# Gated linear attention and a gMLP block on one core: another start of batch 0, one decay exponential and one mask operation per chunk, a new order table

## The chip, the cores and the metric

One core of a Trainium2 chip runs the whole program. It has a matrix engine (TensorE, PE in the profile), three engines for elementwise work (VectorE or DVE, ScalarE or ACT, GpSimd or POOL), and queues for transfers (issued here by SyncE, SP). The metric is the device time of one execution in microseconds. Three runs of the kernel before took 138.06, 138.46 and 139.54 us, so the median is 138.46 us.

## The reference

There are 4 batches, 8 heads, 768 tokens and a head size of 48. An attention with a decaying state comes first, then a gated block with a product along the tokens:

```python
for t in range(S):
    state = alpha[:, :, t, :, None] * state + einsum('bhd,bhe->bhde', k[:, :, t], v[:, :, t])
    y[:, :, t] = einsum('bhd,bhde->bhe', q[:, :, t], state)
x = y.transpose(0, 2, 1, 3).reshape(B, S, H * D)          # [4, 768, 384]
h = maximum(x @ w_in, 0)                                  # [4, 768, 1024]
u, v = h[..., :512], h[..., 512:]
v_n = (v - mean(v)) / sqrt(var(v) + 1e-6)
v_s = einsum('ts,bsd->btd', w_spatial, v_n) + b_spatial[None, :, None]
out = (u * v_s) @ w_out                                   # [4, 768, 384]
```

## The kernel before

The tokens of each batch are cut into 6 chunks of 128, which gives 24 chunks numbered 0 to 23. For one chunk the kernel takes the logarithm of alpha (ACT), sums it along the tokens with triangular matrices of ones (PE), takes exponentials of the sums (ACT), scales k and q with them (POOL and DVE), turns both with PE and copies them out of PSUM (the tile `kqT`), forms the scores of the chunk (PE), multiplies them by the causal mask (DVE, into `ptm`), and forms y from the masked scores, v and the old state (PE). A state update (PE, then DVE and POOL) leads to the next chunk. The decay of a whole chunk is one number per head and feature. PE sums it beside the other sums, and ACT takes its exponential (`ebc`, into `bc` or `bcq`).

Chunks come in three forms. A single chunk has one token in each partition. A pair (`pair`) loads two chunks at once, with two tokens in each partition; a group of four (`four_chunks`) loads four tokens a partition, which makes longer pieces for the transfers. Two tuples say where the forms stand: `PAIRS` and `QUADS` hold numbers of chunk pairs (number j is chunks 2j and 2j+1). Here batch 0 is a group of four followed by a pair, batch 1 a group of four followed by two singles, and batches 2 and 3 are singles.

Behind the attention the x of a chunk (`xT`) meets `w_in`. PE makes u and v, ACT or DVE apply the maximum, DVE takes the statistics of v, a small shift is computed, and ACT or DVE write the normalised `vn`. The spatial product takes `w_spT` and `vn`, DVE adds the bias, POOL multiplies with u, and PE multiplies by `w_out`.

No loop sets the order of this work. Each step is recorded as an operation with its engine, what it needs, and how many PSUM banks it takes. A table of words, `PLAN`, then gives the order in which all of them are issued. `P62@0:512#0` means: operation 62 on PE (D is DVE, A is ACT, G is POOL, S is SyncE), which takes bank 0, with 512 columns of a matmul on constant data issued ahead of it into bank 0 (called junk below). `replay` walks through the table. Each engine works through its own operations in this order, and waits on counters of other engines where data or banks need it. So an instruction that waits holds up everything behind it on its engine.

The eight banks of PSUM are eight tiles before, one for each bank. The lines that the change touches stand below by their numbers in the profile: L836 and L944 are the scores, L843 and L949 the masks, L586 the masks of a pair, L700, L901 and L471 the sums of the decay, L915, L725 and L504 its exponential, L1084 the shift and L1092 and L1096 the normalised v, L178 and L180 copies, L189 and L393 products on DVE or POOL, L1005 the products of the gMLP block, and L242 the junk matmuls.

Of the kernel before, what the change touches and what calls it, by code (L numbers as in the profile page):

```python
# [21 lines left out]
class Op:  # L22


    def __init__(self, key, engs, emit, deps, take, pe):
        self.key, self.engs, self.emit, self.take, self.pe = key, engs, emit, take, pe
        self.deps = [d for d in deps if d is not None]
        self.done = False


class Slot:
# [11 lines left out]
D2 D0 D4 D1 G9 G11 G5 G6 D3 S56 S57 S59 S58 A60 S12 S169 S170 A61 S275 S171 D8 P62@0:512#0:512#0:512#0 P66@1 P67 P63  # L43
P70@2 P71 P74@3 P75 A68 A64 D79 G82 P91@4,5 P52@6 A69 A72 A76 G7 A78 A92 A84 A65 G88 G87 A73 A77 D85 D90 D81 D93 D53
D83 D80 P103@6,4,5,7:512#7:424#7 P94@0,1 D86 D104 D89 D106 G13 P97@6,2:192#2 D98 A95 P100@3,0 D101 A96 P117@3,6:376#1
P115@4,1 A99 G107 G14 A15 A173 D102 D109 P128@0,2 D119 D118 P174@5 A116 A122 A176 P130@6,4 S16 D132 D131 S172 A135
P175@1 A129 P120@3 P54@2 G110 G105 P136@0,4 A121 A178 A55 G111 G108 P133@6 G181 A180 A134 G184 A179 D112 A177 D138
P123@7,3 P141@2 S20 G279 G280 G281 G17 G19 G18 D124 D125 P151@6 P187@7,4 P126@3 S23 S277 S276 D185 A152 A127 G186 G183
G113 G114 D182 P190@5,6 A189 A192 A142 P144@3 D137 P139@4 D188 D191 A140 G22 G21 D153 D143 P199@6,5 P196@2,7 P162@4
A283 A145 P290@0 A163 P154@1 P160@3 A282 A291 A155 D200 D201 D198 D197 D164 P193@4 A161 P156@7 A157 A165 D194 D146  # L50
P158@5 A159 G195 P202@1,2 P203 S26 A204 A147 D166 P293@4 P37@5,7 D38 P34@3,6 G24 S278 S387 S399 G25 S506 S29 D35
P207@1 D148 D208 D36 A39 A292 P205 P284@7 P40@3,5 A206 A285 A167 G10 D42 P210@2 D149 D150 D41 S388 S389 D168 D209 S401
S400 P287@5 P223@6 P219@3 P221@1 A211 A294 A224 A288 D212 A286 A220 A213 D298 D304 A289 A295 D214 D222 D215 A216
P225@6 P233@2 P217@3 P229@7 P237@0 A218 A28 D301 G300 G27 D307 G297 P226 D227 G303 G306 P43@3,5 D45 P230 P234 D231
D235 A296 A44 P46@4,6 P309@5,1 D311 P238 P49@7,3 D50 D51 A48 A47 A310 P312@2,6 P318@1,4 P315@5,7 P249@3 P250 A313 A319
A317 A299 A314 A302 D316 D320 D239 G236 D251 P341@4,1 P335@7,5 P245@0 P246 G305 G308 D336 D342 G232 P321@7,6,3,2 G240
G228 D343 D322 A510 G33 D337 D324 D247 P253@4 P333@7,1 P254 P241@5 P242 G323 A391 A403 A30 A340 A334 A32 G325 P392@0
D255 P348@7,6 D243 D327 D350 A393 P344@4 A394 P338@5 G31 G328 D397 D330 D349 G396 P404@3 A345 A339 A405 A406 P257@1
A395 S495 S390 A258 P260@4 P359@2 S402 G407 G248 G326 G329 S494 S560 P346@0,7 D408 P354@3,5 P410@1,6 A360 D331 A347
A353 A411 D356 D355 P362@2 G252 G398 P351@7 A352 P357@3 D412 S508 S497 S509 P421@6,1 P416@5,0 D361 S496 S507 S562 S550  # L60
S548 S611 S561 S551 S549 A358 A363 D418 D423 P511@7 P369@3 P413@0 P374@2 P380@1 D414 D417 A261 A512 P378@0 D422 A498
D364 A375 A564 P263@5 P499@6 G244 G332 G409 G256 A370 A379 A513 D371 G415 A500 A501 P419@0 P424@3 A425 G517 G505 G503
D381 D382 D516 G515 A420 P266@2 P269@4 A502 A365 A383 A270 D366 D504 P429@0 P426@1 P438@3 P440@6 D384 A368 A430 A427
P436@4 A437 A441 A385 D264 D439 P272@0 D367 D267 D428 D431 D386 P521@1 P372@4 A514 A273 P565@6 P376@2 A377 A432 A552
P442@7 A568 P529@0 D443 D522 P456@3 D433 D434 A435 A566 A567 D373 P452@7 P553@1 P518@2,5 A519 A554 A556 D520 A555 P457
D458 D530 D570 G569 G523 G557 G459 P444@4 P445 P448@5 D446 P453 D454 P468@6 P449 D558 D450 P533@7,4 P524@2,0 P572@1,3
D525 G451 G455 P472@5 P469 P460@2 P473 D526 D534 D535 G531 G447 D474 S623 A559 P575@7 D576 A573 P461 S625 S612 S563
A615 D470 D462 P616@4 P527@5 P536@1 A627 S613 A574 P579@7,3 P588@6,0 G577 A617 A528 D589 A618 A537 P628@5 A629 A571
G475 P538@2 A630 P464@1 S624 S614 S730 S718 S721 S626 S720 G620 D621 D581 D580 S733 S732 P476@6 G631 G578 P541@3
P584@7 A539 A619 A542 P465 S784 S719 A477 D632 P634@5,4 D590 A636 D466 D585 S731 A722 P591@3 S786 S772 S785 S773 S835  # L70
S774 A592 S787 S775 G622 G532 P582@1 A583 D635 D540 P637@7 P482@6 A633 A483 P723@5 G586 G471 D638 G639 A724 P645@3,4
P640@0,2 D543 G463 G587 P479@7 P604@6 P596@1 D646 D642 D641 A734 A726 D647 G729 G467 A605 A741 G727 P593@3 P600@6 A594
# [16 lines left out]

PAIRS = (2,)
QUADS = (0,3)
PLAIN = (0, 2)
IDLE = 16

SPLIT = ()
SMALL = ()


SUMS = (
# [30 lines left out]
def kernel(  # L132
# [134 lines left out]
    def op(key, engs, emit, deps=(), take=(), use=(), pe=None):  # L267
# [3 lines left out]
        for s in list(take) + list(use):  # L271
            s.users.append(o)
# [15 lines left out]
    def zeros(n):  # L288
        def emit(_):
            if n == 0:  # L290
# [5 lines left out]
                for t in bcs:  # L296
                    nc.vector.memset(t, 0.0)
# [967 lines left out]
```

## Time and profile before

| what | value |
|---|---|
| median of three runs | 138.46 us |
| profiled execution, first to last instruction (span) | 137.9 us |
| PE busy | 130.1 us (94%) |
| DVE busy | 120.2 us (87%) |
| ACT busy | 107.7 us (78%) |
| POOL busy | 86.6 us (63%) |
| moved by DMA | 28.66 MB, mean 208 GB/s |

The page gives no own time of the profiled execution beyond its span; the span is the time from its first to its last instruction. It lies 0.56 us below the median of the runs. Busy times are sums over the span, so engines overlap. A group's row holds its line, engine, operation, output and inputs with their shapes, the count, the busy time in us with the mean ns of one instruction, and the idle time of the engine ahead of it.

### The profile page before, as it was taken

What the parts mean: (1) busy time and instruction counts of PE and PEld (TensorE: products, weight loads), DVE (VectorE), ACT (ScalarE), POOL (GpSimd) and SP (SyncE); (2) the same over time, 40 slices, a digit from 0 to 9 for tenths busy, and PEclk for the clock granted to TensorE, in tenths of its full rate; (3) what the DMA queues carried; (4) which work ended last, traced back from release to release, by engine and by line L of the source; (5) the groups of instructions that cost most, each with busy time, mean ns of one, the idle gap of its engine ahead of it and who ended that gap; (6) DMA issues with size and microseconds to landing.
All of it is one profiled execution on the core that took longest, in us unless ns stands there. A gap on an engine that the chain in (4) does not pass through costs nothing.

```text
span 137.9 us, 5298 instructions
## 1 busy us (share of the span) xinstructions
PE 130.1 (94%) x2108; PEld 79.4 (58%) x2122; DVE 120.2 (87%) x300; ACT 107.7 (78%) x261; POOL 86.6 (63%) x146
## 2 busy tenths in 40 slices
PE   6999998999999999799999999999999999999990
PEld 3365555565566556466657676656576765566560
DVE  6259999989989999899899999997999999974960
ACT  3476998999999799699997989999865796953040
POOL 7355899993499799761079989520799841004550
PEclk9999999999999999999999999999999999999999
DMA  3999999499989788699999898999960597101064
GB/s 88 370 372 381 344 349 361 106 373 382 355 162 281 159 168 165 124 186 188 193 204 201 164 209 156 189 186 216 213 134 5 187 349 270 63 0 57 0 233 172
DMA packets 76521, 28.66 MB, mean 208 GB/s; under 512 B 63056, under 2 KB 74960, under 8 KB 76496
## 3 DMA queue, kind: packets, MB, share of 16 engines
q1 hardware_dynamic: 76464, 28.32, 77.8%
q8 instruction: 16, 0.26, 0.8%
q14 instruction: 9, 0.07, 0.2%
q0 software_dynamic: 32, 0.00, 0.0%
HBM read 23.60 MB, written 4.72 MB: 205 GB/s over the span
## 4 chain that ended last, share of the span: by engine, by line
PE 60%; DMA 19%; POOL 8%; issue 3%; SPq 3%; ACT 3%; DVE 0%; POOLq 0%; ACTq 0%
PE bank L1005 43%; DMA raw_w<-in_moe_w_spatial_dram 6%; DMA kc<-in_k_dram 5%; DMA raw_w<-in_moe_w_out_dram 4%; DMA ac<-in_alpha_dram 4%; PE bank L960 3%; SPq L883 3%; PE bank L944 2%; PE bank L988 2%; PE bank L416 2%; POOL w_row L180 2%; POOL kt L189 2%; PE bank L932 1%; PE bank L898 1%; POOL state L189 1%
## 5 line engine op out<-in xcount | busy, mean ns | idle before, releaser
L1005 PE MATMUL bank<-w_spT,vn 128*128 128x384 bf16 x192 | 35.6, 327 | 0.0
L189 POOL TENSOR_TENSOR gT<-vs,uT 128x384 bf16<-128x384 f32 x28 | 25.7, 933 | 14.1 <-DVE vs L1152 14.1
L189 POOL TENSOR_TENSOR kt<-kc,binv 128x384 bf16<-128x384 f32 x22 | 20.2, 928 | 22.3 <-ACT binv L908 15.2
L1005 PEld LDWEIGHTS <-vn 128*128 128x128 bf16 x192 | 17.5, 98 | 11.2 <-issue 0.3
L1005 PE MATMUL bank<-w_in,xT 128*128 128x512 bf16 x58 | 17.4, 380 | 1.6 <-ACT xT L178 0.7
L1005 PE MATMUL bank<-xT,w_in 128*128 128x384 bf16 x96 | 18.7, 326 | 0.0
L1005 PE MATMUL bank<-w_out_sb,gT 128*128 128x384 bf16 (+1 forms) x100 | 18.4, 320 | 0.0
L1152 DVE TENSOR_TENSOR vs<-bank,bsp_bc 128x384 f32<-128x384 f32 x31 | 16.3, 549 | 2.4 <-PE bank L1005 2.3
L949 DVE TENSOR_TENSOR ptm<-bank,mask 128x512 bf16<-128x512 f32 x28 | 17.9, 682 | 0.5 <-PE bank L944 0.3
L178 ACT COPY kqT<-bank 128x512 bf16<-128x512 bf16 (+1 forms) x20 | 15.0, 793 | 3.1 <-PE bank L988 1.9
L1067 DVE BATCH_NORM_STATS2 stats<-v_sb 128x6 f32<-128x512 bf16 x24 | 16.4, 683 | 0.6 <-ACT v_sb L184 0.5
L184 ACT ACTIVATE v_sb<-bank 128x512 bf16<-128x512 f32 x20 | 11.7, 597 | 2.0 <-PE bank L1005 1.7
L184 ACT ACTIVATE uT<-bank 128x384 bf16<-128x384 f32 x27 | 12.4, 494 | 0.7 <-PE bank L1005 0.6
L1005 PEld LDWEIGHTS <-w_in 128*128 128x128 bf16 x96 | 9.0, 97 | 6.7 <-DVE ptm L949 0.3
L189 DVE TENSOR_TENSOR qt<-qc,bank 128x384 bf16<-128x384 f32 x24 | 12.6, 545 | 0.2 <-DMA qc<-in_q_dram 0.2
L1005 PEld LDWEIGHTS <-gT 128*128 128x128 bf16 x100 | 9.2, 98 | 5.8
L178 ACT CAST xT<-bank 128x384 bf16<-128x384 f32 x23 | 10.4, 482 | 1.1 <-PE bank L416 0.8
L843 DVE TENSOR_TENSOR ptm<-bank,mask 128x512 bf16<-128x512 f32 x16 | 10.3, 683 | 0.2 <-PE bank L836 0.2
L242 PE MATMUL bank<-junk 128*128 128x512 f32 (+3 forms) x14 | 8.8, 763 | 1.0 <-DVE junk L1231 1.0
L1005 PEld LDWEIGHTS <-xT 128*128 128x128 bf16 x72 | 6.2, 97 | 6.2 <-ACT xT L178 1.2
L178 ACT COPY raw_w<-bank 128x384 f32<-128x384 f32 x8 | 3.8, 479 | 7.3 <-PE bank L1005 7.2
L393 DVE TENSOR_TENSOR zs<-bank,state 128x384 f32<-128x384 f32 x16 | 8.8, 548 | 0.5 <-PE bank L932 0.4
(162 smaller groups left out, 264.3 us busy)
## 6 DMA issues: line engine op xcount, KB each, us to landing
ac<-in_alpha_dram SPq DMA_DIRECT2D x14, 192.0 KB, 4.4
kc<-in_k_dram SPq DMA_DIRECT2D x14, 192.0 KB, 4.4
qc<-in_q_dram SPq DMA_DIRECT2D x14, 192.0 KB, 4.4
vc<-in_v_dram SPq DMA_DIRECT2D x14, 192.0 KB, 4.2
raw_w<-in_moe_w_spatial_dram SPq DMA_DIRECT2D x3, 768.0 KB, 7.8
out_dram<-raw_w SPq DMA_DIRECT2D x11, 192.0 KB, 2.1
out_dram<-o_sb SPq DMA_DIRECT2D x9, 192.0 KB, 2.0
ac<-in_alpha_dram SPq DMA_DIRECT2D x2, 768.0 KB, 6.7
```

The lines of the kernel that those rows point to most:

```text
L178: nc.scalar.copy(out=out, in_=in_)
L184: nc.scalar.activation(out=out, in_=in_, func=AF.Relu)
L189: ENG[eng].tensor_tensor(out=out, in0=in0, in1=in1, op=ALU.mult)
L242: nc.tensor.matmul(out=banks[n][:, 0:cols].rearrange("p (a b) -> p a b", a=4), lhsT=junk, rhs=junk[:, None, 0:cols // 4].to_broadcast([128 ...
L393: lambda _: nc.vector.tensor_tensor(out=zs[i % 3], in0=tp(), in1=state[(i - 1) % 3], op=ALU.add),
L843: nc.vector.tensor_tensor(out=ptm[n2][:, ci, s], in0=banks[sl.bank].rearrange("p (hp t) -> p hp t", hp=HP), in1=mask[:, 3][:, None, :].to_ ...
L883: nc.sync.dma_start(out=t[x].rearrange("p hp s d -> p (hp s) d"), in_=src[b, :, c * C:c * C + C, :].rearrange("h s d -> s h d"))
L949: nc.vector.tensor_tensor(out=ptm[n2][:, ci, s], in0=banks[sl_p[s].bank].rearrange("p (hp t) -> p hp t", hp=HP), in1=mask[:, 2][:, None, : ...
L960: nc.tensor.matmul(out=place(to, 3 * hp + (0, 1, 1, 2)[x]), lhsT=heads(vb, hp, x), rhs=ptm[n2][:, ci, x // 2, hp, :], start=(turn == 0), s ...
L1005: nc.tensor.matmul(out=ps, lhsT=lhsT, rhs=rhs, start=first and n == 0, stop=last and n == len(pairs) - 1)
L1067: nc.vector.bn_stats(out=stats[tt % 2], in_=v_sb[n2][:, tt, :])
L1152: nc.vector.tensor_tensor(out=vs[d], in0=banks[sl.bank][:, 0:TH], in1=bsp_bc[:, th, :], op=ALU.add)
```

## The change

Eight things change together.

- Batch 0 begins with a pair (chunks 0 and 1), and its other four chunks are one group of four with four tokens a partition: `PAIRS` goes from (2,) to (0,), `QUADS` from (0,3) to (1,3), `PLAIN`, which says how the sums are formed, from (0, 2) to (0, 1). The loads follow this split. Batches 1 to 3 keep their forms.
- The decay of a chunk is laid out on all 128 partitions. A matmul of `own_half` and `off_half` puts -1024 where the entries of the other head belong, so that one exponential gives a zero there; before, two exponentials of 64 partitions wrote the two halves of a tile that held zeros.
- One DVE instruction masks a chunk's scores in both of their banks, with 1024 elements a partition; before, two did 512 each.
- PSUM is one tile of 8 banks, and a bank is a view into it. The mask's operand is the view from the lower bank of the two to the higher, with a step.
- The shift of the layernorm is computed only for slices whose `vn` is written by ACT. That is 2 of 24 by the new table; before ACT wrote 6, and the shift was computed for all 24.
- Memsets of `bc` and `bcq` go, and those of `own_half` and `off_half` come.
- The broadcast of the spatial bias is recorded as needing the sums of chunk pair 0 where it needed those of pair 1.
- The order table is new throughout, with other banks; junk columns go from 3040 to 3600.

```diff
+D47 D48 D50 P227 D228 P302@3,0 P308@2,5 P305@7,4 A303 S271 G229 D306 D307 P242@1 P243 D244 G221 S29 A309 P328@2,4 D329
+P333@7,3 D334 A380 A304 A310 A392 P238@6 P234@0 G292 G298 P235 D236 A295 G301 P314@2,4,5,1 D315 G33 D317 A485 A31 A32
...
-PAIRS = (2,)
-QUADS = (0,3)
-PLAIN = (0, 2)
+PAIRS = (0,)
+QUADS = (1, 3)
+PLAIN = (0, 1)
+FAR = -1024.0
...
-    banks = [pp.tile([128, 512], FP32, name=f"bank{n}") for n in range(8)]
+    psum = pp.tile([128, 8, 512], FP32, name="bank")
+    banks = [psum[:, n, :] for n in range(8)]
...
+    def both_banks(slots):
+
+        lo, hi = (sl.bank for sl in ranked(slots))
+        return psum[:, lo:hi + 1:hi - lo, :]
...
+                nc.vector.memset(own_half.bitcast(FP32), 0.0)
+                nc.vector.memset(off_half, 0.0)
+                for s in range(2):
+                    nc.vector.memset(own_half[32 * s:32 * s + 1, 64 * s:64 * s + 64], 1.0)
+                    nc.vector.memset(off_half[32 * s:32 * s + 1, :, 1 - s:2 - s], FAR)
...
+    def decays(cm, n, parts):
+
+        width = 2 * n * HP
+        nc.tensor.matmul(
+            out=cm[:, DM:DM + width], lhsT=own_half, rhs=off_half[:, 0:n * HP, :].rearrange("p a s -> p (a s)"),
+            start=True, stop=False)
+        of = ones_col if n == 1 else (halves_of if n == 2 else quarters_of).rearrange("p c s -> p (c s)")
+        for hp in range(HP):
+            for x, la in enumerate(parts):
+                nc.tensor.matmul(
+                    out=cm[:, DM + 2 * n * hp:DM + 2 * n * hp + 2 * n], lhsT=la[:, hp].rearrange("p s d -> p (s d)"),
+                    rhs=of, start=False, stop=(hp == HP - 1 and x == len(parts) - 1))
...
             def ebc(_):
-                for s in range(2):
-                    nc.scalar.activation(out=bc[half(s), :, s], in_=banks[sl_c.bank][half(s), DM:DM + HP], func=AF.Exp)
+                nc.scalar.activation(
+                    out=bc, in_=banks[sl_c.bank][:, DM:DM + 2 * HP].rearrange("p (hp s) -> p hp s", s=2), func=AF.Exp)
...
-            for s in range(2):
-                def mk(_, s=s):
-                    nc.vector.tensor_tensor(
-                        out=ptm[n2][:, ci, s], in0=banks[sl_p[s].bank].rearrange("p (hp t) -> p hp t", hp=HP),
-                        in1=mask[:, 2][:, None, :].to_broadcast([128, HP, 128]), op=ALU.mult)
-
-                op(("ms", i, s), "DVE", mk, [("sc", i), ("y", 2 * j - 4), ("y", 2 * j - 3), ("one",)], use=[sl_p[s]])
+
+            def mk(_):
+                nc.vector.tensor_tensor(
+                    out=ptm[n2][:, ci], in0=both_banks(sl_p).rearrange("p s (hp t) -> p s hp t", hp=HP),
+                    in1=mask[:, 2][:, None, None, :].to_broadcast([128, 2, HP, 128]), op=ALU.mult)
+
+            op(("ms", i), "DVE", mk, [("sc", i), ("y", 2 * j - 4), ("y", 2 * j - 3), ("one",)], use=sl_p)
...
             for x in (tt - 1, tt):
+                if engine_of[made[("vn", b, x)].n] != "ACT":
+                    continue
                 nc.vector.tensor_scalar(
...
-        made[("bb", th)].deps.append(made[("cum", 1, 1)])
+        made[("bb", th)].deps.append(made[("cum", 0, 1)])
```

Of the table the diff shows the two new lines with chunks 6 and 7 of batch 1: operation 328 is the scores of chunk 6 in banks 2 and 4 and 329 their mask, 333 and 334 are those of chunk 7 in banks 7 and 3, and 238 is a spatial product into bank 6.

How the instructions stand is shown at three places. In these rows a name ends with the buffer's number in the program; `bank4_68` is bank 4 before, and `bank_64` is the one PSUM tile after. A wait on a counter of another engine stands in brackets.

The first place is the scores of chunks 6 and 7 (`kqT` times `kqT`) on PE and the spatial product (`w_spT` and `vn`) behind them. The kernel before, from the last spatial product ahead of the scores:

```order
L1005 MATMUL bank3_67<-w_spT_90,vn0_140 128x384
L836 LDWEIGHTS kqT1_111 [waits DVE_49]
L836 MATMUL bank4_68<-kqT1_111 128x128 [waits Activation_49]
L836 LDWEIGHTS kqT1_111
L836 MATMUL bank1_65<-kqT1_111 128x128
...
L836 MATMUL bank7_71<-kqT1_111 128x128 [waits Activation_49]
L836 LDWEIGHTS kqT1_111
L836 MATMUL bank5_69<-kqT1_111 128x128
...
L1005 LDWEIGHTS vn0_140
L1005 MATMUL bank0_64<-w_spT_90,vn0_140 128x384 [waits DVE_49]
```

And after, from the end of the scores of chunk 6 to the spatial product:

```order
L850 LDWEIGHTS kqT1_106
L850 MATMUL bank_64<-kqT1_106 128x128
L850 LDWEIGHTS kqT1_106
L850 MATMUL bank_64<-kqT1_106 128x128 [waits DVE_49]
...
L1016 LDWEIGHTS vn0_135
L1016 MATMUL bank_64<-w_spT_85,vn0_135 128x384 [waits DVE_49]
L1016 LDWEIGHTS vn0_135
L1016 MATMUL bank_64<-w_spT_85,vn0_135 128x384
```

Before, the scores of both chunks follow each other with waits on copies that free their banks, and the product behind them waits for an earlier DVE reader of bank 0. After, the first score of chunk 7 waits for DVE, and so does the spatial product into bank 6.

The second place is DVE at the same point: the masks (`ptm`) and what stands around them. The kernel before:

```order
L1152 TENSOR_TENSOR vs2_154<-bank3_67,bsp_bc_88 128x384 [waits PE_49,Pool_49]
L843 TENSOR_TENSOR ptm1_116<-bank7_71,mask_73 128x512 [waits PE_49,Activation_49]
L843 TENSOR_TENSOR ptm1_116<-bank4_68,mask_73 128x512
L843 TENSOR_TENSOR ptm1_116<-bank1_65,mask_73 128x512
L189 TENSOR_TENSOR state0_126<-bank7_71,bcq1_122 128x384 [waits PE_49]
L843 TENSOR_TENSOR ptm1_116<-bank5_69,mask_73 128x512
```

And after:

```order
L1165 TENSOR_TENSOR vs2_149<-bank_64,bsp_bc_83 128x384 [waits PE_49,Activation_49,Pool_49]
L857 TENSOR_TENSOR ptm1_111<-bank_64,mask_66 128x1024 [waits PE_49,Activation_49]
L857 TENSOR_TENSOR ptm1_111<-bank_64,mask_66 128x1024 [waits PE_49]
L1165 TENSOR_TENSOR vs0_147<-bank_64,bsp_bc_83 128x384 [waits PE_49,Activation_49,Pool_49]
L191 TENSOR_TENSOR state0_121<-bank_64,bcq1_117 128x384 [waits PE_49]
```

Four masks of 512 with a state product among them have become two masks of 1024 with nothing between them, and each waits for PE.

The third place is DVE in batch 0, at the masks of chunks 2, 3, 5 and 4 of the changed kernel, with the state's products (`zs`) between them:

```order
L857 TENSOR_TENSOR ptm1_111<-bank_64,mask_66 128x1024 [waits PE_49,Activation_49]
L423 TENSOR_TENSOR zs0_118<-bank_64,state2_123 128x384 [waits Pool_49]
L857 TENSOR_TENSOR ptm1_111<-bank_64,mask_66 128x1024 [waits Activation_49]
L857 TENSOR_TENSOR ptm0_110<-bank_64,mask_66 128x1024 [waits PE_49]
L423 TENSOR_TENSOR zs1_119<-bank_64,state0_121 128x384 [waits Pool_49]
L857 TENSOR_TENSOR ptm0_110<-bank_64,mask_66 128x1024 [waits PE_49,Activation_49]
```

Before, batch 0's group of four was chunks 0 to 3, with eight masks of 512 here:

```order
L843 TENSOR_TENSOR ptm0_115<-bank6_70,mask_73 128x512 [waits PE_49]
L843 TENSOR_TENSOR ptm0_115<-bank3_67,mask_73 128x512
L843 TENSOR_TENSOR ptm1_116<-bank4_68,mask_73 128x512 [waits PE_49,Activation_49]
L843 TENSOR_TENSOR ptm1_116<-bank6_70,mask_73 128x512
L393 TENSOR_TENSOR zs0_123<-bank7_71,state2_128 128x384 [waits Pool_49]
L843 TENSOR_TENSOR ptm1_116<-bank4_68,mask_73 128x512 [waits PE_49]
L843 TENSOR_TENSOR ptm0_115<-bank7_71,mask_73 128x512 [waits PE_49]
L843 TENSOR_TENSOR ptm0_115<-bank3_67,mask_73 128x512 [waits PE_49,Activation_49]
```

The second mask of the changed kernel (chunk 3) waits for ACT, and the others wait for PE or for both.

More of the change, by code (lines that the diff above doesn't have):

```diff
@@ L481, in cum_products @@
                 return
[L482 to L485 removed]
+            decays(cm, 2, [la[:, 1]])
         for par in range(2):
@@ L692, in sums @@
             return banks[sl_c[a].bank][:, 0:DM].rearrange("p (h d) -> p h d", h=H)
-        def tot_view():
-            return banks[sl_c[3].bank][:, DM:DM + 4 * HP].rearrange("p (hp c) -> p hp c", c=4)
-        def totals(cm, parts):
-            for hp in range(HP):
-                for x in parts:
-                    nc.tensor.matmul(
-                        out=cm[:, DM + 4 * hp:DM + 4 * hp + 4], lhsT=la[x][:, hp].rearrange("p s d -> p (s d)"),
-                        rhs=quarters_of, start=(x == parts[0]), stop=(x == 3))
         def cum_products(a):
```

185 lines of the change are left out of this document (86 added, 99 removed).

## The prediction

> **What bounds the kernel now.** The page's first two parts come first: who is busy, and whether that holds along the whole span.
>
> ```profile
> span 137.9 us, 5298 instructions
> PE 130.1 (94%) x2108; PEld 79.4 (58%) x2122; DVE 120.2 (87%) x300; ACT 107.7 (78%) x261; POOL 86.6 (63%) x146
> PEclk9999999999999999999999999999999999999999
> ```
>
> TensorE is busy for 94% of the span at the full granted clock. Next, the busy time of each engine by stretches (start:end, length, then PE first; 6.00 of 6.00 is a stretch without a gap):
>
> ```profile
> 0.00:6.40 6.40, 5.35 (x7) 2.03 (x8) 3.17 (x35) 2.21 (x3) 3.68 (x17) 1.00 0.69 219
> 6.40:16.50 10.10, 9.65 (x195) 5.79 (x194) 7.74 (x17) 8.07 (x19) 6.08 (x11) 1.00 1.11 366
> 16.50:23.00 6.50, 5.96 (x147) 3.61 (x149) 6.50 (x13) 5.96 (x16) 6.34 (x9) 1.00 1.09 350
> 23.00:41.00 18.00, 17.59 (x360) 10.49 (x361) 16.97 (x46) 17.48 (x44) 13.81 (x23) 1.00 0.90 285
> 41.00:47.00 6.00, 6.00 (x118) 3.49 (x114) 5.84 (x12) 5.30 (x13) 5.68 (x9) 1.00 0.92 229
> 47.00:60.00 13.00, 11.79 (x278) 7.66 (x279) 12.11 (x25) 11.12 (x27) 10.53 (x17) 1.00 0.79 153
> 60.00:72.00 12.00, 11.95 (x113) 7.32 (x112) 11.07 (x30) 11.51 (x33) 4.48 (x7) 1.00 1.00 196
> ...
> 88.00:100.00 12.00, 11.89 (x93) 6.99 (x87) 11.04 (x32) 11.42 (x33) 3.87 (x6) 1.00 0.98 199
> 100.00:112.00 12.00, 11.84 (x242) 7.87 (x244) 11.79 (x23) 8.63 (x19) 10.56 (x13) 1.00 0.50 149
> 112.00:130.00 18.00, 17.90 (x218) 10.65 (x209) 14.69 (x38) 10.12 (x26) 3.63 (x5) 1.00 0.29 104
> ```
>
> From 23 to 130 us these stretches leave PE idle for 0.41, 0, 1.21, 0.05, 0.11, 0.16 and 0.10 us, about 2.0 in all. A new microsecond of PE waiting there is therefore a microsecond of time, and no more than 2 us can be won. Up to 23 us it idles for 2.0 us more (1.05, 0.45 and 0.54). The chain of waits still names transfers for a fifth of the span, all early:
>
> ```profile
> PE 60%; DMA 19%; POOL 8%; issue 3%; SPq 3%; ACT 3%; DVE 0%; POOLq 0%; ACTq 0%
> ```
>
> DVE has 0% of it. In the kernel before DVE works beside PE and nobody waits for it for long; whether that stays so decides this case.
>
> **The change part by part.** *The mask operations.* The scores of one chunk go to two banks, and DVE multiplies each by the mask. The rows of the mask and of an operation of the same kind with 384 elements, and the timeline of one place (start, duration; the 16 score products, the products behind them, the masks):
>
> ```profile
> L949 DVE TENSOR_TENSOR ptm<-bank,mask 128x512 bf16<-128x512 f32 x28 | 17.9, 682 | 0.5 <-PE bank L944 0.3
> L393 DVE TENSOR_TENSOR zs<-bank,state 128x384 f32<-128x384 f32 x16 | 8.8, 548 | 0.5 <-PE bank L932 0.4
> 42.09 0.62 PE L836 MATMUL bank<-kqT 48*128 48x128 bf16 x16
> 42.64 1.15 PE L1005 MATMUL bank<-w_spT,vn 128*128 128x384 bf16 x6
> 42.81 1.89 DVE L843 TENSOR_TENSOR ptm<-bank,mask 128x512 bf16<-128x512 f32 x3
> ```
>
> 128 elements more cost 0.134 us (682 against 548), so a mask of 1024 is estimated at 0.682 + 4 x 0.134 = 1.22 us. Between 1.22 and 2 x 0.682 = 1.36 I take 1.22. Three masks in a row took 1.89, so the second adds only 0.605: two separate ones end 1.29 after the first began. Merging 24 pairs thus saves DVE between nothing and 24 x 0.07 = 1.7 us.
>
> The price lies in what stands around the merged mask. Before, PE went on at 42.64, while DVE masked from 42.81 on. Now the eight banks are one tile, and the mask's operand is a view from the lower bank to the higher with a stride. The waits that the rows of the changed order show fit only if that view counts as everything from its lowest to its highest bank. So a mask on banks 2 and 4 also waits for whoever is filling bank 3, and the next product into bank 3 waits for the mask. Before, with a tile for each bank, neither wait existed. The bank numbers in the order table give the places. A **full stop** is one where PE's very next work is such a product, or where the mask waits for the product just ended and PE's next work needs the mask. Its price at the place above: the mask would start at 42.81, end 1.22 later at 44.03, and PE stand from 42.64: 1.39 us.
>
> Seven are full stops (bank pair of the mask in brackets): chunk 2 [0,4], where the copy of turned queries from bank 2 waits for the mask, and the products that turn v need that bank; chunk 5 [0,4], which holds up a u product into bank 3; chunk 4 [2,6], which waits for y of chunk 5 in bank 5, and y of chunk 4 needs it; chunk 6 [2,4], which holds the scores of chunk 7 in [3,7]; chunk 7 [3,7], which holds a spatial product into bank 6; chunk 9 [4,7], which waits for y of chunk 8 in bank 5, and y of chunk 9 comes next; chunk 13 [1,7], which holds the scores of chunk 12 in [4,5]. Behind the standing product PE's whole queue stands, as rows of the order show it at chunks 6 and 7. 7 x 1.39 = **9.7 us**.
>
> Four more stops involve an ACT operation or two masks:
>
> ```profile
> L178 ACT CAST xT<-bank 128x384 bf16<-128x384 f32 x23 | 10.4, 482 | 1.1 <-PE bank L416 0.8
> L178 ACT COPY kqT<-bank 128x1024 bf16<-128x1024 bf16 x9 | 9.0, 1016 | 2.0 <-PE bank L988 1.9
> L908 ACT ACTIVATE binv<-bank 128x384 bf16<-128x384 f32 x14 | 7.0, 498 | 0.9 <-PE bank L901 0.7
> L1005 PE MATMUL bank<-w_spT,vn 128*128 128x384 bf16 x192 | 35.6, 327 | 0.0
> ```
>
> Chunk 3 [2,6] waits for the x copy out of bank 3 (0.48), and a v product into bank 5 waits for the mask. One v half of three 512-wide matmuls lies between, at 35.6/192 x 512/384 = 0.25 each: 0.48 + 1.39 - 0.74 = 1.1. Chunk 8 [0,6] waits for a copy of 1.02 out of bank 2, with two chunks of scores beside it (0.55, from 42.09 to 42.64): 1.9. Chunk 11 [0,7] waits for an exponential (0.50) on bank 5, and u into bank 0 follows: 1.9. Chunks 16 and 17 run one behind the other ahead of a u product into bank 5: 1.39 + 1.22 = 2.6. Together 7.5. Four small ones (chunk 19 before the sums of chunk 23, chunk 21 before y of 20, chunk 14, and batch 0's first pair) I put at 0.5, 0.4, 0.3 and at most 1.0, 2.2 together. Here the ACT work may be done already, since ACT runs ahead while PE stands elsewhere; so I count half of both, **3.8 and 1.1**, with nothing and the full 9.7 as ends.
>
> The Trainium skill ("Perfetto Trace Analysis", section "Optimizing Scalar/DVE Operations") holds that larger operations pay where the engine is saturated, and that breaking instructions up may finish work sooner where an unsaturated engine causes bubbles on others. DVE at 87% with 0% of the chain is the second case: by that rule the merge goes the wrong way, by the other 1.7 us of DVE time would come back; the trace of before can't show the merged form.
>
> *The decay.* One matmul of 8 to 32 columns comes to each of 14 chunks' or groups' sums, and one exponential replaces two.
>
> ```profile
> 9.05 0.54 PE L700 MATMUL bank<-quarters_of,la 128*128 128x4 bf16 x16
> L915 ACT ACTIVATE bc<-bank 64x4 f32<-64x4 f32 x22 | 3.7, 169 | 0.6 <-DVE qt L189 0.3
> ```
>
> Sixteen such narrow products take 0.54, or 0.034 each: 14 x 0.034 = 0.5 on PE; eight state update products fewer give back 0.3, so **+0.2**. ACT saves 14 x 0.169 = 2.4 us, which isn't on the path. What hides it there is PE's own work; were ACT the bound, it would gain that.
>
> *The layernorm's shift.* It is computed only for the 2 slices left on ACT, and four slices move to DVE.
>
> ```profile
> L1084 DVE TENSOR_SCALAR shift<-mvs,rstd 128x1 f32<-128x1 f32 x24 | 3.9, 204 | 1.2 <-ACT rstd L1078 1.2
> L1096 DVE TENSOR_SCALAR vn<-v_sb,mvs,rstd 128x512 bf16<-128x512 bf16 x18 | 6.9, 404 | 0.0
> L1092 ACT ACTIVATE vn<-v_sb,shift,rstd 128x512 bf16<-128x512 bf16 x6 | 4.9, 815 | 0.2 <-DVE shift L1084 0.2
> ```
>
> DVE: -22 x 0.204 (or 0.16, by 3.9/24) + 4 x 0.404 = -2.9; ACT: -4 x 0.815 = -3.3. Both lie beside PE and count nothing. The moved memsets, and the bias row's broadcast that waits for other sums, fall in the start.
>
> *Batch 0 and the order.* The transfers are issued in another order (half-size alpha, k and q of the pair first), and 2296 junk columns stand before the first sums instead of 1536.
>
> ```profile
> 1.05 5.49 PE L242 MATMUL bank<-junk 128*128 128x512 f32 x6 [1.05 <-DVE junk L1231]
> 6.37 0.39 PE L717 MATMUL bank<-la,le_quad 128*128 128x384 bf16 x1
> 10.18 1.84 PE L242 MATMUL bank<-junk 128*128 128x512 f32 x4
> ```
>
> 1536 junk columns took 5.49; 760 more take 1.5 at the rate of the later 936 columns (1.84) or 2.7 at the first one's. The first sums then begin at 7.9 to 9.1 us instead of 6.37. In return two sums stand first instead of four, and 1304 junk columns follow later instead of 1504. The ends are -2.0 (all early idling gone) and +2.7; I take 0, as the transfers in total and the work up to the first v are the same. For the later order I take the 2.0 us of PE idling between 23 and 130 us as won, since the stops let the other engines run ahead of PE: **-2.0**; at worst nothing is won.
>
> The Trainium skill ("TensorE: Matmul & The Clock Gate", section "Part 1: The HAM clock gate") says that PE runs at half rate until a window of about 3.4 us was busy, and cools again after an idle one. The first junk at 0.92 us per piece and the later at 0.46 agree in size; stops of 1.4 to 2.6 us are shorter than such a window, so by it the clock stays.
>
> The sum: 9.7 + 3.8 + 1.1 + 0.2 + 0 - 2.0 = **+12.8**. The profiled execution had 137.9 from its first to its last instruction; the median of the runs is 138.46, 0.56 above, which I keep: 137.9 + 0.56 + 12.8 = 151.3, rounded to 151.
>
> **The rivals.** *Half price.* If the new order has PE waiting for the mask's true reader at these places anyway, or DVE starts the masks earlier than I assume, only the seven full stops at half price stay: 138.46 + 4.9 + 0.2 = 143.6, with 141 to 146 around it. Against it: at six of the seven the next work lies right behind the scores or y, where before had none of these waits.
>
> *Full price.* All stops in full and nothing won: 138.46 + 9.7 + 7.5 + 2.2 + 0.2 = 158.1. It decides if ACT is not ahead; its 78% speak against.
>
> *Faster.* The waits bind nobody, because the masks are done before PE reaches the next product: DVE has 1.7 + 2.9 = 4.6 us less work, ACT 5.7 less, so masks start at once. Then PE wins its idling, 2.0 from 23 us on and up to 1.0 at the start: 138.46 + 0.2 - 3.0 = 135.7. It takes that the stops cost less than two us in all, one and a half of the twenty. The 1.22 us that even an idle DVE needs speak against.
>
> *No change.* The stops cost just what the order wins, 1.4 to 4 us: 137 to 140. That one tile and merged masks do nothing for the waits is excluded by the rows of the order.
>
> **How the numbers follow.** Forecast (146 to 157): 0.60. Half price: 0.20. Full price or more: 0.08. Faster: 0.08. No change: 0.04. The range is 141 to 158: the forecast's own, all of half price, and the lower edge of full price, some 0.84. About 1% is what a measurement of this kernel can tell from no change. Faster by more 0.08, within 0.04, slower 0.88.
>
> **What would show it.** In the profile after, PE's waits should name DVE masks (their lines) with 12 to 20 us in 10 to 15 stretches of 1 to 2.6 us, where before they name DVE only for the junk's memset; the merged mask should take near 1.22 us; PE's idling should lie right behind scores of chunks 4 to 9 and 11 to 17; granted clock 1.00. I am wrong if PE's waits for masks sum to under 4 us, if the mask takes far less than 1.2, or if the first 23 us differ by more than 3 us.

## The result, and the profile after

The changed kernel takes 179.4 us (median; 179.04 to 181.49) where the kernel before took 138.9 in the same comparison. The ratio is 1.297, with a 95% interval of 1.288 to 1.306. The direction was forecast, the size was not: 151 us, with 141 to 158 as the range. The difference of 40 us has four parts, which the experiments below take apart. They sum to 40.9, since the kernel before took 138.56 in the comparison of the last row.

| part | measured as | us |
|---|---|---|
| waits of the merged masks, and the clock that falls with them | changed kernel less the same with split masks: 179.40 - 148.62 | 30.8 |
| the new order, with its bank numbers and batch 0's form (and the one PSUM tile, the bias broadcast's other condition and 560 more junk columns) | split kernel less the order before with the new decay and shift: 148.62 - 141.51 | 7.1 |
| load buffers that start at another address | 141.51 - 139.14 | 2.4 |
| decay, shift and memsets themselves | 139.14 - 138.56 | 0.6 |

The page of the changed kernel, its first parts, the chain and the rows of the masks:

```profile
span 178.0 us, 5249 instructions
PE 145.3 (82%) x2130; PEld 85.5 (48%) x2130; DVE 125.0 (70%) x261; ACT 102.9 (58%) x239; POOL 87.1 (49%) x147
PEclk9999955557999699798799999999999996999999
PE 65%; DVE 19%; ACT 8%; issue 4%; DVEq 0%
L960 DVE TENSOR_TENSOR ptm<-bank,mask 128x1024 bf16<-128x1024 f32 x14 | 16.8, 1220 | 9.7 <-ACT binv L919 2.9 <-PE bank L955 2.3 <-ACT kqT L180 2.1
L857 DVE TENSOR_TENSOR ptm<-bank,mask 128x1024 bf16<-128x1024 f32 x8 | 9.8, 1223 | 17.4 <-PE bank L446 9.2 <-ACT xT L180 4.4 <-PE bank L850 2.6
```

DVE, which had 0% of the chain before, has 19%. PE stands for 32.7 us (178.0 less 145.3) where it stood for 7.8, which is 24.9 more. It is also busy for 15.2 us longer with nearly the same instructions. The row of the clock shows the main reason, with 5 in four slices where it had 9 throughout; 560 more junk columns are a smaller one. A merged mask takes 1.22 us, as estimated.

PE's waits in the changed kernel (engine, output and line, what it waited for, total us, times, longest):

```profile
PE bank L1016 <- DVE ptm L960: 7.0, 3, 2.5
PE bank L1016 <- DVE ptm L857: 6.2, 4, 2.8
PE bank L868 <- DVE ptm L857: 2.8, 2, 1.4
PE bank L828 <- ACT kqT L180: 2.0, 1, 2.0
PE bank L971 <- DVE ptm L960: 1.8, 2, 1.5
PE bank L850 <- DVE ptm L857: 1.5, 1, 1.5
PE bank L955 <- DVE ptm L960: 1.4, 1, 1.4
PE bank L912 <- DVE ptm L960: 1.1, 1, 1.1
PE bank L583 <- DVE ptm L609: 0.7, 1, 0.7
```

The rows that name masks sum to 22.5 us; before, no row of PE's waits named one. The 2.0 us for a copy of `kqT` are the stop at chunk 2, where that copy waits for the mask. The timeline at chunks 6 and 7, first DVE and then PE, shows a stop from both sides:

```profile
57.07 1.21 DVE L857 TENSOR_TENSOR ptm<-bank,mask 128x1024 bf16<-128x1024 f32 x1
58.78 1.22 DVE L857 TENSOR_TENSOR ptm<-bank,mask 128x1024 bf16<-128x1024 f32 x1 [0.49 <-PE bank L850]
```

```profile
56.39 0.40 PE L850 MATMUL bank<-kqT 48*128 48x128 bf16 x8
58.34 0.40 PE L850 MATMUL bank<-kqT 48*128 48x128 bf16 x8 [1.55 <-DVE ptm L857]
60.05 1.44 PE L1016 MATMUL bank<-w_spT,vn 128*128 128x384 bf16 x4 [1.31 <-DVE ptm L857]
```

The scores of chunk 6 end at 56.79, their mask at 58.28, and only then do the scores of chunk 7 begin, though they take other banks. Their mask ends at 60.00, and the spatial product begins at 60.05.

In this trace the clock changes only on a fixed grid of 3.41 us: cut along it, every stretch runs at 0.50 or at 1.00. Some of them (PE's busy time first, the granted clock third from the end):

```profile
18.44:21.85 3.41, 2.35 (x100) 1.79 (x97) 3.41 (x9) 1.89 (x5) 2.37 (x4) 1.00 1.04 383
21.85:25.26 3.41, 1.40 (x38) 0.79 (x28) 2.29 (x4) 1.05 (x2) 2.91 (x6) 0.50 0.77 234
...
69.64:73.05 3.41, 0.78 (x4) 0.38 (x4) 1.25 (x2) 1.32 (x2) 3.31 (x6) 1.00 0.71 138
73.05:76.46 3.41, 3.41 (x30) 1.86 (x31) 0.00 (x0) 1.58 (x4) 0.00 (x0) 0.50 1.03 198
76.46:79.88 3.42, 2.02 (x75) 1.44 (x64) 2.62 (x4) 1.61 (x5) 1.01 (x2) 1.00 0.64 129
...
117.42:120.84 3.42, 1.39 (x11) 0.78 (x11) 2.44 (x3) 1.19 (x5) 2.09 (x3) 1.00 1.14 224
120.84:124.25 3.41, 3.41 (x84) 2.16 (x82) 2.26 (x6) 2.78 (x9) 0.01 (x1) 1.00 0.14 28
...
144.73:148.14 3.41, 0.97 (x11) 0.36 (x12) 2.48 (x3) 1.40 (x2) 1.38 (x2) 1.00 0.00 0
148.14:151.56 3.42, 3.42 (x75) 2.53 (x76) 2.08 (x3) 0.96 (x2) 0.50 (x1) 0.50 0.02 5
```

A stretch in which PE stood for 1.06 us (18.44) or 2.63 us (69.64) is followed by one at half clock. One with 2.03 us of standing (117.42) is not, so the time stood is not the whole rule. In all, ten stretches, 34 us, ran at half clock, and PE was busy for 27.3 us in them; if half speed doubles the time of this work, that is some 13.6 of the 15.2 us (an estimate from these stretches).

### The profile page after: what moved, and what is told of

It reads as the page before. It is cut to its first block, busy times and chain, and to the rows that moved or that the text cites. A ratio compares the mean times of both kernels' runs of the same rounds, so it can differ in the third digit from the quotient of the medians.

```text
span 178.0 us, 5249 instructions
## 1 busy us (share of the span) xinstructions
PE 145.3 (82%) x2130; PEld 85.5 (48%) x2130; DVE 125.0 (70%) x261; ACT 102.9 (58%) x239; POOL 87.1 (49%) x147
## 4 chain that ended last, share of the span: by engine, by line
PE 65%; DVE 19%; ACT 8%; issue 4%; DVEq 0%
PE bank L1016 42%; DVE ptm L960 6%; DVE ptm L857 6%; PE bank L246 5%; PE bank L971 3%; ACT kqT L180 3%; PE bank L446 2%; PE bank L955 2%; PE bank L999 2%; PE bank L868 1%; ACT v_sb L186 1%; DVE zs L423 1%; DVE qt L191 1%; ACT vb L180 1%; PE bank L912 1%
## 5 line engine op out<-in xcount | busy, mean ns | idle before, releaser
L1016 PE MATMUL bank<-w_spT,vn 128*128 128x384 bf16 x192 | 36.8, 336 | 1.5 <-DVE ptm L857 1.3
L191 POOL TENSOR_TENSOR gT<-vs,uT 128x384 bf16<-128x384 f32 x29 | 26.7, 937 | 21.4 <-DVE vs L1165 21.4
L191 POOL TENSOR_TENSOR kt<-kc,binv 128x384 bf16<-128x384 f32 x23 | 21.0, 923 | 25.8 <-ACT binv L919 15.2
L1016 PE MATMUL bank<-xT,w_in 128*128 128x384 bf16 x96 | 21.1, 350 | 6.3 <-DVE ptm L960 4.9
L1016 PE MATMUL bank<-w_in,xT 128*128 128x512 bf16 x72 | 22.3, 435 | 3.5 <-DVE ptm L857 3.5
L180 ACT COPY kqT<-bank 128x512 bf16<-128x512 bf16 (+1 forms) x21 | 16.0, 795 | 14.4 <-DVE ptm L857 5.6
L960 DVE TENSOR_TENSOR ptm<-bank,mask 128x1024 bf16<-128x1024 f32 x14 | 16.8, 1220 | 9.7 <-ACT binv L919 2.9
L857 DVE TENSOR_TENSOR ptm<-bank,mask 128x1024 bf16<-128x1024 f32 x8 | 9.8, 1223 | 17.4 <-PE bank L446 9.2
L186 ACT ACTIVATE v_sb<-bank 128x512 bf16<-128x512 f32 x22 | 13.0, 603 | 13.6 <-PE bank L1016 13.5
L1078 DVE BATCH_NORM_STATS2 stats<-v_sb 128x6 f32<-128x512 bf16 x24 | 16.4, 683 | 3.6 <-ACT v_sb L186 3.4
L186 ACT ACTIVATE uT<-bank 128x384 bf16<-128x384 f32 x23 | 11.2, 491 | 7.7 <-PE bank L1016 7.7
L182 POOL CAST sbd<-state 128x384 bf16<-128x384 f32 x13 | 6.8, 530 | 12.8 <-DVE state L191 12.7
L1109 DVE TENSOR_SCALAR vn<-v_sb,mvs,rstd 128x512 bf16<-128x512 bf16 x22 | 9.8, 480 | 0.0
```

The lines of the kernel that those rows point to most:

```text
L180: nc.scalar.copy(out=out, in_=in_)
L182: ENG[eng].tensor_copy(out=out, in_=in_)
L186: nc.scalar.activation(out=out, in_=in_, func=AF.Relu)
L191: ENG[eng].tensor_tensor(out=out, in0=in0, in1=in1, op=ALU.mult)
L857: nc.vector.tensor_tensor(out=ptm[n2][:, ci], in0=both_banks(sl_p).rearrange("p s (hp t) -> p s hp t", hp=HP), in1=mask[:, 3][:, None, Non ...
L960: nc.vector.tensor_tensor(out=ptm[n2][:, ci], in0=both_banks(sl_p).rearrange("p s (hp t) -> p s hp t", hp=HP), in1=mask[:, 2][:, None, Non ...
```

## The experiments

**Splitting the masks** again in the changed kernel, with all else kept (one of three places):

```diff
-                nc.vector.tensor_tensor(
-                    out=ptm[n2][:, ci], in0=both_banks(sl_p).rearrange("p s (hp t) -> p s hp t", hp=HP),
-                    in1=mask[:, 2][:, None, None, :].to_broadcast([128, 2, HP, 128]), op=ALU.mult)
+                for s, sl in enumerate(ranked(sl_p)):
+                    nc.vector.tensor_tensor(
+                        out=ptm[n2][:, ci, s], in0=banks[sl.bank].rearrange("p (hp t) -> p hp t", hp=HP),
+                        in1=mask[:, 2][:, None, :].to_broadcast([128, HP, 128]), op=ALU.mult)
```

> The changed kernel, with each merged mask split again into two operations of 512, one for each bank; the order table, the one PSUM tile, the decay, the shift and batch 0's form stay as changed. Theory S (the merged mask's operand counts as all banks from its lower to its higher; PE stands behind masks for 22.5 us, and these stops bring stretches at half clock, about 15 us more): PE's waits for masks fall below 3 us, the granted clock is 0.98 or more, 136 to 142 us. Rival O (the new order and start of batch 0 are slow in themselves): 165 us or more.

It took 148.62 us (ratio 1.072, 1.068 to 1.075), with a granted clock of 0.958. PE waited 0.3 us for masks instead of 22.5, in one row:

```profile
PE bank L973 <- DVE ptm L962: 0.3, 1, 0.3
```

So the merge accounts for 30.8 us on these banks. PE stands 22.0 us less (10.7 of a span of 146.8) and is busy for 9.2 us less (136.1 against 145.3) with the same 2130 products. But 148.62 lies above what theory S expected, and the clock below it, so the theory was incomplete: 10 us have another cause.

**Merging the masks in the kernel before**, on its own order and banks: one PSUM tile, and one mask of 1024 where the first of the two stood.

```diff
-    banks = [pp.tile([128, 512], FP32, name=f"bank{n}") for n in range(8)]
+    psum = pp.tile([128, 8, 512], FP32, name="bank")
+    banks = [psum[:, n, :] for n in range(8)]
...
+                    if made[("ms", i, 0)].done or made[("ms", i, 1)].done:
+                        return
```

> The kernel before with its own order, banks, decay and shift, but with PSUM as one tile and each chunk's mask as one operation of 1024, issued where the first of the two stood. Theory S: PE waits for masks for 10 us or more, the granted clock falls below 1 in places, 155 to 185 us. Rival O: the order of before is kept, so within 2 us of before.

A single run took 161.4 us, with a granted clock of 0.964. PE's waits for masks are 16.4 us over their seven longest rows (6.9, 2.5, 1.6, 1.4, 1.4, 1.3, 1.3). By this run the merge costs 23 us in the order before, too.

**Neighbouring banks**, first in the changed order. The order of operations is the same and the masks stay merged, but the banks are numbered so that the two of each chunk's scores stand side by side, with none in between. Only the bank numbers in the table change; for chunks 6 and 7 the order is still scores, mask, scores, mask.

> The changed kernel with merged masks and the same order of operations, but other bank numbers, so that the two banks of each chunk's scores are neighbours and no bank lies between them. Theory S: as e1, 135 to 141 us, granted clock 0.98 or more. Rival M (a mask of 1024 is itself too long an operation, whatever its banks): 165 us or more, as changed. Rival O: 165 us or more.

152.87 us (1.102, 1.098 to 1.106), and the longest of PE's waits is now for a copy of u:

```profile
PE bank L1016 <- ACT uT L186: 2.5, 2, 1.9
```

26.5 us are gone although every mask is still one operation of 1024. That falsifies rival M: most of the merge's price hangs on the banks and not on the length of the operation. Theory S's 135 to 141 us are missed as well. Next the same on the order before:

> The kernel before with its own order of operations and merged masks over one PSUM tile (as the second experiment), but with other bank numbers, so that the two banks of each chunk's scores are neighbours. Theory S (only the banks in between make the merged mask dear): 137 to 142 us. Rival M (the longer operation is itself dear): 150 us or more.

148.89 us, between the two theories. Here and in the run ahead of it the renumbering could be to blame as well as the longer operation. So the same bank numbers were tried with split masks, on both orders. On the changed order:

> The changed order with the bank numbers of the neighbours' experiment (152.87 us with merged masks), but with each mask split in two (148.62 us with the changed kernel's own banks). Theory M2 (the merged mask itself costs some 4 us there, since both banks come free only after 1.22 us): 147.5 to 149.5 us. Rival B (my other bank numbers cost them, by waits for copies that free a bank late): 151.5 us or more.

152.60 us, against 152.87 with merged masks. Rival B holds and M2 falls on this order: the merge costs 30.8 us over the changed kernel's own banks and 0.3, within the noise, over neighbours. So it is the banks in between that make it dear. The new numbers cost 4.0 us over the changed kernel's own. On the order before:

> The kernel before, unchanged but for the bank numbers of the neighbours' experiment on its order (148.89 us with merged masks). Theory M2: 138 to 140 us, the whole 10 us are the merged mask's. Rival B: 146 us or more, the bank numbers cost them.

145.75 us, just short of rival B's bound. The numbers alone cost 7 us there, and the merged masks 3.1 more (148.89), so here a merged mask on neighbouring banks isn't free: PE's waits for masks sum to 2.8 us with it and to 0.6 with split masks. Bank numbers alone were worth 4 to 7 us.

**Junk in the stops** of the changed kernel. Seven words of the table get junk ahead of them, for instance:

```diff
-P160@2,6
+P160@2,6:512#5:256#5
...
-P333@7,3
+P333@7,3:384#1
```

> The changed kernel with 2240 more junk columns, ahead of seven of the products that stand behind masks or copies early on (about 17 to 40 us and near 58 us), into banks outside the masks' ranges. They fill part of the stops with work and shorten none. Theory S with the clock falling because PE stands: the half-clock stretch from 22 to 42 us shrinks or goes, and the time falls by 4 to 10 us although work was added. Rival C (the clock falls for another reason, such as the load): no shorter, 179 to 184 us.

The pieces sum to 2752 columns, not to 2240. A single run took 174.4 us, 5 below the changed kernel, with a clock of 0.98 instead of 0.904; PE's waits for masks were still above 19 us. PE was busy for 143.5 us instead of 145.3 although it did more. More work made the kernel faster and kept the clock up, which speaks for theory S (the clock falls because PE stands) and against rival C, as far as one run can.

**Junk at the start of the split kernel**, where its half-clock stretch lies (1664 columns ahead of four products):

```diff
-P145@3,7
+P145@3,7:512#0:256#0
```

> The split kernel (first experiment) with 1664 more junk columns, ahead of four products between 16 and 25 us, where PE stands for some 3 us and the clock is halved from 19 to 29 us. Theory K (a good part of the 10 us that are left is that half-clock stretch, and it comes from PE standing): the granted clock is 1.00 throughout and the time 143 to 146 us. Rival L (the stretch costs nothing, since PE then waits for loads and POOL anyway): 148 to 150 us, even where the clock stays up.

149.49 us (1.077, 1.073 to 1.082) at a clock of 0.98 in the profiled run and 0.994 to 0.998 in the other three. The clock was mostly up and the time not lower. That is rival L's figure, and theory K's is not reached; the junk's own time may have eaten a gain, some 1.5 us (an estimate from four pieces with 936 columns that took 1.84 us in the kernel before).

**One scaling of k from POOL to DVE** in the split kernel:

```diff
-G133
+D133
```

> The split kernel with one of batch 0's four scalings of k for the group of four moved from POOL to DVE, just ahead of DVE's scalings of q. PE stood there for 1.46 us (at 16.9 to 18.4 us) while POOL did three of them in 2.87 us. Theory P (POOL's row of scalings sets the start in the new order): PE's stop falls to 0.7 us or less, the time to 146.5 to 148 us, less if the clock then isn't halved. Rival Q (the loads of q set it, which DVE waits for): within 0.5 us of the split kernel, 148.1 to 149.1 us.

147.88 us, 0.7 below the split kernel and at the edge of theory P; PE's stop fell to some 1.1 us, not to 0.7. The runs overlap (146.91 to 148.46 against 147.71 to 148.94), so POOL's row of scalings is at most a small part.

**Decay and shift on the order before.** The order table, the tuples, the eight bank tiles and the masks of 512 are those of before; the decay, the shift and the memsets are the new ones.

> The kernel before with its order, its eight bank tiles and masks of 512, but with the single decay exponential, the shift only where ACT writes vn, and the changed memsets. Theory O2 (what is left beyond the stops is the new order and batch 0's form): 137.5 to 139.5 us. Rival D (the decay's extra product and its longer operands cost it): 141 us or more.

141.51 us (1.021, 1.017 to 1.024). The figure is rival D's; its cause is not, as the next two runs show. From 41 to 130 us PE stands no longer than before (0.2 us against 1.7), but the first sums wait for alpha's load, which lands 0.6 us later; the first half of `w_in` lands 1.65 us later. The loads of this kernel are slower with the same packets. Its two new constants take 320 bytes a partition ahead of the load buffers. Counted from the sizes of the tiles ahead of them (no profile shows an address), those started at a multiple of 512 bytes before, and now start 320 bytes behind one. A spare tile of 192 bytes puts them back:

```diff
     off_half = consts.tile([128, 16, 2], BF16, name="off_half")
+    spare = consts.tile([128, 96], BF16, name="spare")
+    nc.gpsimd.memset(spare[:, 0:2], 0.0)
```

> The kernel before with the new decay and shift (as the earlier experiment that took 141.51 us), plus a spare tile of 192 bytes a partition behind the new constants, so that the load buffers start at a multiple of 512 bytes again, as before; without it they start 320 bytes behind one. Theory A (the 320 bytes of the two new constants move the load buffers, and loads into them run at 325 instead of 370 GB/s early on): 365 GB/s or more between 4 and 12 us, 137.5 to 139.5 us. Rival D (the decay's own work costs it): 141 us or more, whatever the rate.

139.14 us (1.005, 1.002 to 1.008). And a spare tile of 320 bytes in the kernel before, which changes nothing but addresses:

```diff
+    spare = consts.tile([128, 160], BF16, name="spare")
+    nc.gpsimd.memset(spare[:, 0:2], 0.0)
```

> The kernel before, unchanged but for a spare tile of 320 bytes a partition ahead of the load buffers, which moves them as the change does. Theory A: 320 to 335 GB/s between 6 and 12 us where it was 368 to 392, and 140.5 to 142.5 us. Rival D: as before, 138 to 139.5 us.

140.78 us (1.014, 1.011 to 1.017). The stretches from 6 to 10 us, with GB/s last: the kernel before, the one with only its buffers moved, the one with decay and shift, and the one with decay, shift and buffers put back. Of the second, the profiled run took 143.38 us where the other six took 140.5 to 141.0; the third has the same buffers, took 141.63 in its profiled run and 141.1 to 142.2 in the others, and shows the same rates.

```profile
6.00:8.00 2.00, 2.00 (x11) 0.96 (x10) 0.00 (x0) 1.43 (x3) 0.00 (x0) 1.00 1.10 368
8.00:10.00 2.00, 2.00 (x41) 1.43 (x39) 1.47 (x2) 1.65 (x5) 1.75 (x3) 1.00 1.09 371
```

```profile
6.00:8.00 2.00, 1.54 (x9) 0.87 (x9) 0.00 (x0) 1.43 (x3) 0.00 (x0) 1.00 1.11 325
8.00:10.00 2.00, 2.00 (x41) 1.42 (x38) 1.38 (x2) 1.66 (x5) 1.66 (x3) 1.00 1.11 327
```

```profile
6.00:8.00 2.00, 1.02 (x6) 0.57 (x6) 0.00 (x0) 1.58 (x2) 0.00 (x0) 1.00 1.11 325
8.00:10.00 2.00, 2.00 (x26) 1.32 (x24) 0.86 (x1) 1.66 (x4) 1.20 (x2) 1.00 1.11 326
```

```profile
6.00:8.00 2.00, 1.60 (x10) 0.92 (x10) 0.00 (x0) 1.43 (x3) 0.00 (x0) 1.00 1.10 368
8.00:10.00 2.00, 2.00 (x42) 1.45 (x40) 1.44 (x2) 1.63 (x5) 1.72 (x3) 1.00 1.10 373
```

The DMA engines are as busy in all four (1.09 to 1.11 in the column ahead of GB/s), and move 12% less where the buffers start 320 bytes off. Theory A holds. The Trainium skill ("DMA: Bandwidth & Descriptors", section "How a descriptor splits into AXI transactions") says that a transaction must start at a multiple of 256 bytes, and that for a piece which doesn't start there the first one begins below it and carries bytes that aren't used. It says so of reads; the direction agrees with these rows (325 against 368 GB/s), where it is the destination that moved. That it is the same mechanism is not shown.

**The split kernel with the spare tile**, and then with the scaling on DVE as well:

> The split kernel (148.62 us) with the spare tile of 192 bytes, so that its load buffers start at multiples of 512 bytes again. Theory A: loads between 6 and 12 us at 340 GB/s or more where they ran at 300, the start of the gMLP products 1 to 3 us earlier, 144.5 to 147 us. What is left over 139 us is then the order's. Rival: the slow early loads are due to the smaller loads of the pair alone, 148 to 149 us.

146.69 us (1.057, 1.052 to 1.062), 1.9 below the split kernel and within theory A's range. Its other signs did not come: the early rates are 295 to 346 GB/s instead of 340 or more, and the first product of x with `w_in` begins at 27.6 us where it began at 26.9.

> The split kernel with the spare tile and with one scaling of k moved to DVE (the earlier experiment without the spare tile took 147.88 us). Theory A and P together: 143 to 146 us, 0.5 to 1.5 below the split kernel with the spare tile alone. Rival: no gain on top of the spare tile.

146.41 us, no clear gain on top: three runs lay at 146.4 to 147.1, with mean clocks of 0.958 to 0.975, and one at 142.8 with 0.998. That one run is a sign that the half-clock stretch costs some 3.6 us; the junk in the split kernel spoke against it. From that kernel two last runs asked what the order costs at its start:

> The split kernel with the spare tile and one scaling of k on DVE (146.41 us; three of its four runs took 146.4 to 147.1, one 142.8), plus 896 junk columns in four pieces ahead of products between 17 and 24 us. Theory K (a half-clock stretch from 20 to 31 us costs some 3.5 us, and single runs escape it): the granted clock is 1.00 throughout and the median 142 to 144 us. Rival L (the stretch costs nothing): 146 us or more.

148.03 us (146.37 to 148.96 over six runs, at clocks of 0.974 to 0.988). In the profiled run, 146.37 us at 0.988, the stretch at half clock shrank from three windows to one, and the time did not fall. That is rival L's figure; but the clock was not 1.00 throughout, and the 896 junk columns cost PE some time, so theory K is not confirmed and not tested to the end.

```diff
-P61@0:512#0:512#0:512#0:512#0:248#0
+P61@0:512#0:512#0
```

> The same kernel (146.41 us) with 1024 instead of 2296 junk columns ahead of the first sums. Theory J (the junk holds up the start: the first sums begin at 7 to 8 us, though the logarithm of alpha is done by 5.1 us): the first sums begin at 5.2 us, 144 to 145.5 us. Rival G (the loads of the group of four set the start): within 0.7 us of 146.4, or longer where the clock suffers.

145.06 us (1.044, 1.040 to 1.049). The first sums begin at 5.08 us instead of 7.29, and the median is 1.35 us lower, as theory J has it. But the runs overlap (144.5 to 147.1 against 142.8 to 147.1), so the gain is likely and not shown. Where the order's cost lies, the stretches show: first the split kernel with the spare tile, then the order before with the same decay and shift and its buffers put back.

```profile
0.00:30.00 30.00, 25.32 (x405) 14.16 (x405) 18.98 (x66) 17.29 (x36) 17.05 (x40) 0.84 0.82 257
30.00:60.00 30.00, 29.92 (x587) 18.21 (x589) 27.93 (x63) 28.02 (x67) 23.41 (x35) 0.99 0.96 259
60.00:90.00 30.00, 29.34 (x493) 17.95 (x481) 29.10 (x59) 22.89 (x58) 19.36 (x27) 1.00 0.98 192
90.00:120.00 30.00, 29.45 (x486) 18.43 (x483) 28.40 (x59) 23.21 (x57) 20.43 (x27) 1.00 0.52 114
```

```profile
0.00:30.00 30.00, 26.81 (x520) 15.20 (x522) 23.91 (x78) 22.34 (x49) 23.00 (x48) 1.00 0.93 301
30.00:60.00 30.00, 29.97 (x598) 18.27 (x596) 28.47 (x63) 27.72 (x68) 24.64 (x37) 1.00 0.96 239
60.00:90.00 30.00, 30.00 (x479) 19.40 (x478) 28.48 (x64) 26.16 (x64) 18.51 (x25) 1.00 0.96 188
90.00:120.00 30.00, 29.95 (x464) 18.69 (x463) 27.94 (x61) 23.67 (x57) 15.42 (x19) 1.00 0.64 175
```

From 30 to 120 us PE stands for 1.3 us in the new order and 0.1 in the other. In the first 30 us the new order runs 405 products where the other runs 520, at a mean clock of 0.84, and DVE, ACT and POOL do 5 to 6 us less each. The first product of x with `w_in` begins at 27.6 us there, at 24.1 with less junk, and at 19.7 in the kernel before. So most of the order's 7 us lie in the start. Of its causes the junk (1.35 us) and POOL's scalings (0.7) are pointed at by differences within the spread of the runs. What share the later loads of the group of four, the bank numbers and the clock have stays open.

## Why the prediction was wrong

**The mechanism was right.** The view of the merged mask waits for every bank between its two, PE stands behind DVE, and at the places named. The seven full stops were put at 9.7 us; they measured 2.01, 1.41, 1.40, 1.55, 1.31, 1.40 and 1.38, or 10.5. The merged mask's 1.22 us was right. Three steps failed, each worth 9 to 10 us, and one term was missing.

**Counting half of the partial stops was the first failed step.** The four with an ACT operation or two masks measured 0.68, 2.82, 2.39 and 2.48, or 8.4 us, where 7.5 stood and 3.8 was counted. The idea that ACT would be ahead of PE was wrong for chunks 3, 8 and 11: ACT was busy right up to the operation that the mask waited for, and the mask began 0.03 us after that ended, at 29.01, 70.99 and 82.49 us. The fourth place (2.48) has no ACT operation and came near its full price of 2.6. The small stops, some at places that I had not named, came to 5.7 us instead of 1.1. All stops together are 24.5 us, where the sum had 14.6.

**"By it the clock stays" was the second.** I compared each stop with a window of 3.4 us and let the clock be. The rows show half clock behind windows in which PE stood for about a third of the time or more, and ten windows at half clock. PE's busy time rose by 15.2 us, of which 9.2 go with the split; the sum had nothing for it. The rule of the Trainium skill that I named ("TensorE: Matmul & The Clock Gate", section "Part 1: The HAM clock gate") speaks of an idle window; here none of the windows ahead of a fall was idle throughout.

**"I take 0" for the start and -2.0 for the order was the third.** They were bounded by -2.0 and +2.7 and by nothing won; the order measured +7.1, most of it in the first 30 us. The junk did not hold up the first sums by as much as I feared: in the changed kernel they begin at 6.84 us, not at 7.9 to 9.1. What came late lies behind them. I compared transfers in total, and didn't ask when the group's loads come behind the pair's, and what PE can do until then. Which of these makes up the 7.1 us stays open.

**The addresses were missing altogether.** No part of the working looked at what new constants do to the buffers behind them: 2.4 us. The decay itself, with its 0.2, came near the 0.6 that is left with shift and memsets.

**The rivals.** "Full price" (158) came nearest, 21 us short, and lacked the clock, the start and the addresses. "Faster" and "no change" are out: the order before was no faster with DVE busy for 118.2 us instead of 120.2 (139.14 us against 138.56). The Trainium skill ("Perfetto Trace Analysis", section "Optimizing Scalar/DVE Operations") says that larger operations pay where the engine is saturated. The runs on neighbouring banks agree: the merge won nothing there, with 152.87 against 152.60 us on the changed order and 148.89 against 145.75 on the order before.

## What to carry to other kernels

An operand that strides over several buffers may wait for everything between its ends, so give the parts that are read together neighbouring places, or read them apart; where PE is the bound, look in the issued order for waits right behind the products that fill the operand. Stops of 1 to 3 us on PE can cost more than their sum, since the clock may be halved for the next 3.4 us; here 22.0 us of standing came with 9.2 us of longer work. When small constants are added ahead of load buffers, look at where the buffers now start.

## What the runs showed of the hardware that was not expected

- The granted clock changed only on a fixed grid of 3.41 us in the changed kernel's trace, and half clock can follow a window in which PE stood for as little as 1.06 us; a window with 2.03 us was not followed by it, so another measure than the time stood is at work, which these runs don't show.
- Moving the load buffers by 320 bytes a partition lowered the rate of the early loads from 368 to 325 GB/s with the same 76521 packets, and cost the kernel 2.2 us.
- Junk products in stops can shorten a kernel: 2752 more columns took 5 us off the changed kernel in a single run.
